# Idle products in four early attention tiles, one evacuation moved up, and Strassen products half a step later, in a fused attention and SwiGLU kernel

## The chip, the cores and the metric

One core of one Trainium2 chip runs the whole program. The metric is the device time of one launch in microseconds. Five launches of the kernel before took 358.25 to 359.82 us, with a median of 358.79 us.

## The reference

The reference is sliding-window attention with a linear bias, followed by a SwiGLU block. There are 8 batches of 8 heads, 576 tokens and 64 channels per head; the block has width 512 and inner width 1536.

```python
scores = scale * q @ k.T
mask = (rel >= 0) & (rel < 128)
scores = where(mask, scores - slope[h] * |rel|, -1e9)
attn = softmax(scores)
x = (attn @ v).transpose(0, 2, 1, 3).reshape(4608, 512)
g = x @ w_gate
out = ((g * sigmoid(g)) * (x @ w_val)) @ w_out
```

## The kernel before

**Work and stages.** The tokens are cut into 36 tiles of 128 queries ("units"): four groups of two batches with nine units each, the ninth unit holding the last 64 tokens of both batches. For a unit, q and k of a 128-token rank are brought into transposed form (`kT`, `qT`), TensorE makes the scores (`products`, L254; L282 for narrow ones), ScalarE takes the exponential (L259, L286), VectorE multiplies by a table that holds both the bias and the mask (L263, L290), TensorE multiplies by v with a column of ones appended (`weighted`, L314), and VectorE divides by the sum (L316, L317). The result is transposed on TensorE (L340) and copied by ScalarE (L341) into `xT`; from unit 24 on a DMA transposes it.

The block then works on nine groups of 512 tokens. For each of twelve slices of the inner width there is a gate product `pg` and a value product `pv` (both L363), a tanh on ScalarE (L374), and two VectorE operations that make `uu` (L376) and `hT` (L380). Group 0 and the last group are projected by plain products (L393, L409). Groups 1 to 7 are projected by a Winograd form of Strassen's method: 7 block products instead of 8. It needs sums of slices of h (`sums`, L451 to L454, VectorE, made from the ninth slice of a group on) and sums of the output weights. Its seven products (L472) come in the order A11·B11, A12·B21, S2·T2, S1·T1, S3·T3, S4·B22, A22·T4; A stands for quarters of h, S for sums of h. Two halves X and Y of one PSUM bank receive six of them; VectorE (`half_plus`, L476) or ScalarE reads a half after the products that complete it. There are two calls of seven products for each group, so 14 calls in all.

**What sets the order.** The head of the program (`first_tiles`: four units, then three slices of group 0 over their first 384 tokens) and the first steps of the block after it are in an order written out by hand for TensorE, VectorE and ScalarE. After that a scheduler orders the instructions of each engine from their priorities. `ffn` counts half steps: number 2m is the gate product of slice m, 2m+1 the value product. The set `AT` says after which half steps of a group one Strassen product of the group before is placed; before, it is 2 to 8 and 10 to 16.

**The head, and what the change touches in it.** The pool with the tag `gv` has three PSUM banks. They are used in turn by the transposed k tiles of the head, by the two halves of `av` of the units 0 to 3, and by the first block products. The transposes of q use one further bank. `REPEAT` gives how often a transposition of a head tile is carried out into the same bank; the repetitions change nothing in the result. `idle` is a piece of zeros in `kT` (L99) that serves as an operand for products whose results are overwritten, `busy(7)` starts the kernel with seven of them (L135). `transposes_to(n)` carries out the transpositions (L201) and evacuations (L206) up to the n-th in a fixed list; the fifth entry of the list, index 4, is q of rank 2, the third q tile. `run(scores(0))` goes through unit 0's steps: 0 is the products, 1 the first exponential, 2 the second one with the first masking multiply, 3 and 4 the same for the other four heads.

**Loads.** GpSimd's queue issues the loads of q, k, v and the weights in one fixed sequence, in which a load waits until the load eight places earlier has landed. From rank 9 on q and k are transposed by DMAs on SyncE's queue (L222).

Of the kernel before, what the change touches and what calls it, by code (L numbers as in the profile page):

```python
# [16 lines left out]
P = 128  # L17
# [6 lines left out]
ENGINES = {"all": None, "compute": {ET.PE, ET.DVE, ET.Activation}, "pe": {ET.PE}}  # L24
WARM = 7
IDLE = {("k", 0): 0, ("q", 0): 2}
REPEAT = {("q", 1): 4, ("k", 1): 4, ("q", 2): 3}
FIRST = 4
LEAD = 6
PRE = 0  # L30
# [4 lines left out]
def slot(h):  # L35

    return 4 * (h // 4) + 2 * (h % 2) + (h % 4) // 2
# [9 lines left out]
def kernel(  # L47
# [10 lines left out]
    nc = tc.nc  # L58
# [30 lines left out]
    def first_masks():  # L89
        nc.vector.tensor_copy(idf, idm)  # L90
        for h in sorted(range(H), key=slot):
            nc.scalar.activation(reg[:, slot(h), :], dist, AF.Exp, scale=-(2.0 ** (-8.0 * (h + 1) / H)))
# [5 lines left out]
    idle = kT[:, NK - 1].rearrange("p j t -> p (j t)")  # L98
# [82 lines left out]
    def transposed(name, rank):  # L181
# [16 lines left out]

        for _ in range(REPEAT.get((name, rank), 2) if rank < FIRST else 1):
            for j in range(4):  # L200
# [25 lines left out]
    def scores(i):  # L226

        s, p = units[i]
        def combined(n):
            return scores_128(s, (3, 7, 8)[n], 8, (s, "c", n), msk[n])  # L230

        def together(one, two):
            return [one[0] + two[0]] + one[1:] + two[1:]

        if p == 8:
            return together(combined(1), combined(2))
        if p == 7:
            return together(scores_128(s, p, p, (s, p), reg[:, :, 0:P]), combined(0))
        if p == 3:
            return scores_128(s, p, p, (s, p), reg[:, :, 0:P])  # L240
        ks = (9 * s + p) % NK
        banks = []
        e = epool.tile([P, H, 256], FP16, name="ex", tag="ex", bufs=4)
        ex[(s, p)] = e

        def products():
            for q4 in range(2):
                two = [ps_a.tile([P, 2, 256], FP32, name="ps", tag="a") for _ in range(2)]
                banks.append(two)
                for j in range(2):  # L250
                    pair = 2 * q4 + j
                    for par in range(2):
                        rows = slice(64 * par, 64 * par + 64)
                        nc.tensor.matmul(two[par][:, j, :], kT[rows, ks, pair, :],  # L254
                                         qT[rows, p:p + 2, pair, :], start=(j == 0), stop=(j == 1))

        def act(q4, par):
            o = 4 * q4 + 2 * par
            nc.scalar.activation(e[:, o:o + 2, :], banks[q4][par], AF.Exp, scale=scale)  # L259

        def mul(q4):
            o = slice(4 * q4, 4 * q4 + 4)
            nc.vector.tensor_mul(e[:, o, :], e[:, o, :], reg[:, o, :])  # L263

        return [[products], [lambda: act(0, 0)], [lambda: act(0, 1), lambda: mul(0)],
                [lambda: act(1, 0)], [lambda: act(1, 1), lambda: mul(1)]]
# [27 lines left out]
    def weighted(i):  # L294

        s, p = units[i]
        x = xpool.tile([P, H, D], FP16, name="x", tag="x")
        xs[i] = x
        for half in range(2):
            pool, tag = (ps_f, "gv") if i < FIRST else (ps_a, "a")  # L300
            av = pool.tile([P, 4, D + 1], FP32, name="av", tag=tag)
            todo = []
            for j in range(4):
                h = 4 * half + j
                if p == 8:
                    for n, kt in enumerate((3, 7, 8)):
                        todo.append((j, ex[(s, "c", n)][:, slot(h), :], va[9 * s + kt][:, h, :]))
                else:
                    if p not in (0, 4):
                        todo.append((j, ex[(s, p - 1)][:, slot(h), 128:256],  # L310
                                     va[9 * s + p - 1][:, h, :]))
                    todo.append((j, ex[(s, p)][:, slot(h), 0:128], va[9 * s + p][:, h, :]))
            for n, (j, w, val) in enumerate(todo):
                nc.tensor.matmul(av[:, j, :], w, val, start=(n == 0), stop=(n == len(todo) - 1))  # L314
            rec = xpool.tile([P, 4, 1], FP32, name="rec", tag="rec", bufs=4)
            nc.vector.reciprocal(rec, av[:, :, D:D + 1])  # L316
            nc.vector.tensor_mul(x[:, 4 * half:4 * half + 4, :], av[:, :, 0:D],  # L317
                                 rec.broadcast_to([P, 4, D]))
# [8 lines left out]
    def x_transposed(i):  # L327
        n, j = place(i)
        if n not in xT:
            xT[n] = bpool.tile([P, NKB, 512], FP16, name="xT", tag="xTc" if n == 8 else "xT",  # L330
                               bufs=1 if n == 8 else 3)
        x = xs.pop(i).rearrange("p h d -> p (h d)")
        dst = xT[n][:, :, j * P:(j + 1) * P]
        if i >= X_DMA_FROM:
            nc.sync.dma_start_transpose(dst, x)
            return
        pool, tag, n = (ps_f, "po", 1) if i < FIRST else (ps_a, "a", 4)
        pt = pool.tile([P, NKB, P], FP16, name="px", tag=tag, bufs=n)
        for kb in range(NKB):
            nc.tensor.transpose(pt[:, kb, :], x[:, kb * P:(kb + 1) * P], idm if i < FIRST else idm2)  # L340
        nc.scalar.copy(dst, pt)  # L341
# [13 lines left out]
    def wide(n, m, which, c1=512):  # L355

        w, ms = wg_sb if which == "g" else wv_sb, slice(m * P, (m + 1) * P)
        ps, c0 = early.pop((n, m, which), (None, 0))
        if ps is None:
            pool, tag = (ps_a, "a") if (n, m, which) in OTHER else (ps_f, "gv")  # L360
            ps = pool.tile([P, 512], FP32, name="p" + which, tag=tag)
        for kb in range(NKB):
            nc.tensor.matmul(ps[:, c0:c1], w[:, kb, ms], xT[n][:, kb, c0:c1],  # L363
                             start=(kb == 0 and c0 == 0), stop=(kb == NKB - 1 and c1 == 512))
        if c1 < 512:
            early[(n, m, which)] = (ps, c1)
        return ps
# [136 lines left out]

    AT = {*range(2, 9), *range(10, 17)}

    def ffn():

        for n in range(NBLK):
# [6 lines left out]
            for m in range(NMB):  # L518
                for half, _ in enumerate(gate_val(n, m)):
                    yield 1.0  # L520
                    if n > 1 and 2 * m + half in AT:
                        next(parts)
# [25 lines left out]
    def transposes_to(n):  # L548
        nonlocal done_t
        while done_t < n:  # L550
            transpose(done_t)
            done_t += 1
# [7 lines left out]
    def run(steps):  # L560
        for fs in steps:
            for f in fs:
                f()
            yield

    def first_tiles():

        first_masks()
        transposes_to(need[0] + 1)
        for n, _ in enumerate(run(scores(0))):  # L570
            if n == 2:
                transposes_to(need[1])
        for i in range(FIRST):
            if i + 1 < FIRST:
                for n, _ in enumerate(run(scores(i + 1))):
                    if n == 0 and i + 2 < FIRST:
                        transposes_to(need[i + 2])
            weighted(i)
            if i > 0:
                x_transposed(i - 1)  # L580

        for m, which in ((0, "g"), (0, "v"), (1, "g")):
            wide(0, m, which, 384)
        x_transposed(FIRST - 1)
        for m, which in ((1, "v"), (2, "g"), (2, "v")):
            wide(0, m, which, 384)

    def attention():

        transposes_to(need[FIRST])  # L590
        for _ in run(scores(FIRST)):
            yield FIRST
        for i in range(FIRST, last + 1):
            if i < last:
                transposes_to(need[i + 1])
                for _ in run(scores(i + 1)):
                    yield i
            weighted(i)
            yield i
            loads_to(i + 7)  # L600
            ahead(i)
            yield i
            x_transposed(i)
            yield i
            yield i + 1
# [110 lines left out]
```

## Time and profile before

| | |
|---|---|
| median of five launches | 358.79 us (358.25 to 359.82) |
| the profiled launch | 360.06 us |
| span of the profile, first to last instruction | 358.3 us |
| outside the span | 1.8 us |
| TensorE busy in the span | 341.1 us, 95% |
| VectorE, ScalarE, GpSimd busy | 271.4, 177.7, 106.9 us |
| idle time of TensorE that a named producer ended, 0 to 26 us | 6.4 us |
| the same, 97 to 345 us | 1.6 us |

The profile counts from the first instruction. PE is TensorE, PEld its weight loads, DVE VectorE, ACT ScalarE, POOL GpSimd and SP SyncE; a q behind a name means the engine's queue, which issues DMAs. A number in square brackets behind a row is the engine's idle time before it, with the producer that ended the idle time. Matmuls are pipelined and their ends are modelled, so starts are more exact than ends.

### The profile page before, as it was taken

How to read it: one execution, taken by the hardware profiler on the slowest of the kernel's cores; microseconds unless marked ns; L12 is line 12 of the kernel's file. 1: busy time of each engine (PE TensorE's matmuls, PEld its weight loads, DVE VectorE, ACT ScalarE, POOL GpSimd, SP SyncE). 2: the span in 40 equal slices, each digit the busy share in tenths (PEclk: the TensorE clock that was granted, in tenths of full speed). 3: DMA queues.
4: the chain of work that ended last, by engine and by line, in shares of the span. 5: the costliest groups of instructions: out<-in, count | busy, mean ns of one | idle time of the engine just before them, and what ended most of it. 6: DMA issues, size and time to landing. Idle time of an engine off the chain costs nothing.

```text
span 358.3 us, 7133 instructions
## 1 busy us (share of the span) xinstructions
PE 341.1 (95%) x2701; PEld 193.8 (54%) x2701; DVE 271.4 (76%) x594; ACT 177.7 (50%) x351; POOL 106.9 (30%) x132
## 2 busy tenths in 40 slices
PE   7788997999999999999999999999999999999995
PEld 3544453444456655665466655654665566456543
DVE  4747975898887699777987998789877955975540
ACT  4726784455656455555565454555554333332321
POOL 8954753466728283664300001000000000000000
PEclk9989999999999999999999999999999999999999
DMA  9999999999999999999962224212021201101104
GB/s 150 171 187 186 171 177 100 147 143 147 167 145 177 163 143 180 170 196 112 170 66 79 42 74 32 78 26 75 15 76 29 75 0 60 59 2 59 59 16 103
DMA packets 159939, 37.87 MB, mean 106 GB/s; under 512 B 150432, under 2 KB 155424, under 8 KB 159904
## 3 DMA queue, kind: packets, MB, share of 16 engines
q0 software_dynamic: 116224, 18.62, 81.8%
q1 hardware_dynamic: 43232, 18.49, 27.7%
q8 instruction: 21, 0.34, 0.4%
q10 hardware_dynamic: 448, 0.30, 0.3%
q14 instruction: 14, 0.11, 0.1%
HBM read 37.91 MB, written 9.44 MB: 132 GB/s over the span
## 4 chain that ended last, share of the span: by engine, by line
PE 76%; DVE 12%; ACT 5%; DMA 3%; issue 2%; SPq 0%; ACTq 0%; DVEq 0%
PE pg L363 23%; PE pv L363 22%; PE po L472 14%; PE ps L254 4%; PE av L314 3%; DVE uu L376 2%; PE po L393 2%; PE p L472 2%; DVE hT L380 2%; DVE ex L263 2%; ACT exc L286 2%; PE px L340 2%; DMA qT<-qn 2%; ACT tt L374 1%; ACT ex L259 1%
## 5 line engine op out<-in xcount | busy, mean ns | idle before, releaser
L374 ACT ACTIVATE tt<-pg 128x512 f16<-128x512 f32 x108 | 64.8, 602 | 108.9 <-PE pg L363 102.9
L363 PE MATMUL pg<-xT,wg_sb 128*128 128x512 f16 (+2 forms) x444 | 116.3, 376 | 1.0 <-ACT xT L341 0.7
L363 PE MATMUL pv<-xT,wv_sb 128*128 128x512 f16 (+2 forms) x444 | 113.8, 375 | 1.2 <-DVE uu L376 1.2
L376 DVE SCALAR_TENSOR_TENSOR uu<-tt,pg 128x512 f16<-128x512 f16 x107 | 73.0, 683 | 39.0 <-ACT tt L374 38.4
L380 DVE TENSOR_TENSOR hT<-uu,pv 128x512 f16<-128x512 f16 x108 | 73.7, 683 | 6.0 <-PE pv L363 2.6
L363 PEld LDWEIGHTS <-wg_sb 128*128 128x128 f16 x444 | 41.8, 98 | 38.6 <-issue 4.4
L363 PEld LDWEIGHTS <-wv_sb 128*128 128x128 f16 x444 | 41.4, 98 | 38.9 <-issue 5.6
L259 ACT ACTIVATE ex<-ps 128x512 f16<-128x512 f32 x96 | 50.0, 608 | 9.5 <-PE ps L254 9.4
L168 POOL DMA_DIRECT2D va<-in_v_dram x40 | 34.3, 868 | 42.0 <-PE av L314 35.3
L174 POOL DMA_DIRECT2D qn<-in_q_dram x39 | 33.6, 864 | 40.2 <-DMA qT<-qn 24.0
L174 POOL DMA_DIRECT2D kn<-in_k_dram x39 | 33.4, 860 | 25.8 <-DMA kT<-kn 21.4
L472 PEld LDWEIGHTS <-hT 128*128 128x128 f16 x336 | 32.1, 98 | 14.9 <-issue 1.0
L263 DVE TENSOR_TENSOR ex<-ex,m_reg 128x1024 f16<-128x1024 f16 x48 | 32.8, 686 | 8.4 <-ACT ex L259 8.3
L472 PEld LDWEIGHTS <-S 128*128 128x128 f16 x252 | 23.9, 98 | 12.7 <-issue 4.1
L317 DVE TENSOR_TENSOR x<-av,rec 128x256 f16<-128x256 f32 x72 | 28.6, 420 | 0.4
L286 ACT ACTIVATE exc<-psc 128x512 f16<-128x512 f32 x40 | 21.0, 603 | 5.7 <-PE psc L282 5.7
L472 PE MATMUL po<-T,hT 128*128 128x256 f16 x168 | 22.9, 272 | 0.1
L472 PE MATMUL po<-T,S 128*128 128x256 f16 x168 | 22.9, 273 | 0.0
L314 PE MATMUL av<-va,ex 128*128 128x65 f16 x384 | 20.7, 193 | 2.2 <-DVE x L317 1.3
L314 PEld LDWEIGHTS <-ex 128*128 128x128 f16 x384 | 18.1, 97 | 6.3 <-DVE x L317 2.0
L254 PE MATMUL ps<-qT,kT 64*128 64x256 f16 x192 | 18.0, 272 | 3.3 <-DMA qT<-qn 1.7
L341 ACT COPY xT<-px 128x512 f16<-128x512 f16 x24 | 14.0, 585 | 12.5 <-PE px L340 12.5
(72 smaller groups left out, 284.0 us busy)
## 6 DMA issues: line engine op xcount, KB each, us to landing
out_dram<-osb SPq DMA_DIRECT2D x32, 256.0 KB, 2.7
va<-in_v_dram POOLq DMA_DIRECT2D x32, 128.0 KB, 8.3
qn<-in_q_dram POOLq DMA_DIRECT2D x31, 128.0 KB, 7.5
kn<-in_k_dram POOLq DMA_DIRECT2D x31, 128.0 KB, 8.4
wo_sb<-in_moe_w_out_dram POOLq DMA_DIRECT2D x2, 768.0 KB, 9.3
wg_sb<-in_moe_w_gate_dram POOLq DMA_DIRECT2D x2, 512.0 KB, 10.5
wv_sb<-in_moe_w_val_dram POOLq DMA_DIRECT2D x2, 512.0 KB, 12.2
out_dram<-osb SPq DMA_DIRECT2D x6, 128.0 KB, 2.3
```

The source lines that it names most:

```text
L168: nc.gpsimd.dma_start(va[rank][p0:p1, :, 0:D], src)
L174: nc.gpsimd.dma_start(t_[p0:p1], src)
L254: nc.tensor.matmul(two[par][:, j, :], kT[rows, ks, pair, :], qT[rows, p:p + 2, pair, :], start=(j == 0), stop=(j == 1))
L259: nc.scalar.activation(e[:, o:o + 2, :], banks[q4][par], AF.Exp, scale=scale)
L263: nc.vector.tensor_mul(e[:, o, :], e[:, o, :], reg[:, o, :])
L314: nc.tensor.matmul(av[:, j, :], w, val, start=(n == 0), stop=(n == len(todo) - 1))
L317: nc.vector.tensor_mul(x[:, 4 * half:4 * half + 4, :], av[:, :, 0:D], rec.broadcast_to([P, 4, D]))
L363: nc.tensor.matmul(ps[:, c0:c1], w[:, kb, ms], xT[n][:, kb, c0:c1], start=(kb == 0 and c0 == 0), stop=(kb == NKB - 1 and c1 == 512))
L374: nc.scalar.activation(tt, pg, AF.Tanh, scale=0.5)
L376: nc.vector.scalar_tensor_tensor(out=uu, in0=tt, scalar=one if (n, m) == PIN else 1.0, in1=pg, op0=ALU.add, op1=ALU.mult)
L380: nc.vector.tensor_mul(hT[n][:, m, :], uu, pv)
L472: nc.tensor.matmul(dst, a[:, m, cols], b[:, m, :], start=(start and m == 0), stop=(m == HM - 1), skip_group_check=True)
```

## The change

It has three parts.

1. In `weighted`, units 1, 2 and 3 get two more products into each of their two `av` banks before the real ones, with the zeros as both operands, 256 columns each: 12 products. Their results are overwritten.
2. In the head, `REPEAT` becomes 2 for k of rank 1 (from 4) and 4 for q of rank 2 (from 3), and q of rank 2 is transposed and evacuated after step 0 of unit 0 instead of after step 2. On TensorE the place stays the same (behind the products of unit 0); on VectorE the evacuation now stands ahead of both masking multiplies of unit 0 instead of between them.
3. `AT` becomes 2, 3, 5 to 9 and 11 to 17: in the first call the two products that use no sums stay, and the other five come half a step later; the whole second call comes half a step later.

```diff
-REPEAT = {("q", 1): 4, ("k", 1): 4, ("q", 2): 3}
+REPEAT = {("q", 1): 4, ("k", 1): 2, ("q", 2): 4}
...
             av = pool.tile([P, 4, D + 1], FP32, name="av", tag=tag)
+            if 0 < i < FIRST:
+
+                for _ in range(2):
+                    nc.tensor.matmul(av.rearrange("p j d -> p (j d)")[:, 0:256], idle[:, 0:P],
+                                     idle[:, 0:256], start=True, stop=True)
...
-    AT = {*range(2, 9), *range(10, 17)}
+    AT = {2, 3, *range(5, 10), *range(11, 18)}
...
         for n, _ in enumerate(run(scores(0))):
-            if n == 2:
+            if n == 0:
                 transposes_to(need[1])
```

In the built programs TensorE's order is otherwise the same up to the first Strassen call; from there the scheduler places both the Strassen products and the attention pieces among the block products differently. The loads up to q of rank 10 and the SyncE queue up to its transposition have the same order in both.

## Prediction

> **What bounds the kernel now.** I read the page first, then the granted clock by windows, then the chain of waits and the TensorE rows of the places it names. The page:
>
> ```profile
> PE 341.1 (95%) x2701; PEld 193.8 (54%) x2701; DVE 271.4 (76%) x594; ACT 177.7 (50%) x351; POOL 106.9 (30%) x132
> PEclk9989999999999999999999999999999999999999
> DMA  9999999999999999999962224212021201101104
> ```
>
> TensorE is the bound, but not everywhere: it idles in the first 26 us, one digit of its clock is below 9, and the DMA engines are full for the first half of the span. The windows (busy time by engine, then clock, DMA share, GB/s):
>
> ```profile
> 17.82:21.24 3.42, 2.04 (x32) 1.32 (x33) 3.23 (x12) 1.61 (x4) 1.82 (x3) 1.00 2.07 169
> 21.24:24.65 3.41, 3.05 (x10) 1.43 (x10) 0.42 (x1) 0.31 (x1) 2.71 (x4) 0.50 1.62 193
> 58.78:62.19 3.41, 1.68 (x11) 0.67 (x10) 0.15 (x1) 1.18 (x2) 2.56 (x3) 1.00 0.62 69
> ```
>
> From 21.24 to 24.65 us the clock was half. VectorE is the busy engine just before (3.23 of 3.42 us). The chain shows what half a clock costs: the same four products of 384 columns,
>
> ```profile
> 23.04 1.28 PE pv L363 x4
> ...
> 26.07 0.65 PE pg L363 x4
> ```
>
> The first row lies in the half-clock window, the second after it: 0.32 us against 0.16 us a product.
>
> The decisive place is later. TensorE's rows (start, duration, what, idle time before and its releaser), and SyncE's queue:
>
> ```profile
> 59.10 0.81 PE L393 MATMUL po<-wo_sb,hT 128*128 128x512 f16 x3
> 61.64 0.27 PE L254 MATMUL ps<-qT,kT 64*128 64x256 f16 x1 [1.73 <-DMA qT<-qn]
> ```
> ```profile
> 53.04 1.30 SPq L222 DMA_TRANSPOSE qT<-qn  x1
> 54.40 1.25 SPq L222 DMA_TRANSPOSE kT<-kn  x1
> 55.84 1.19 SPq L222 DMA_TRANSPOSE qT<-qn  x1
> ```
>
> At 61.64 TensorE stands 1.73 us for q of rank 10, whose DMA transposition was issued at 55.84. The chain names a ScalarE exponential before that issue, but the instruction does not use it: its load was issued at 47.22 and took 8.5 us by the DMA view, so it landed at about 55.7. That load stood in GpSimd's sequence behind others, each released by the landing of an earlier load. So this wait ends at a time that the DMA stream sets, whatever the engines do before it. TensorE runs its instructions in order, and this product stands at the same place in the changed program. I call 61.64 the **join**.
>
> **Part 2, the third q tile.** VectorE's rows:
>
> ```profile
> 9.36 0.42 DVE L206 COPY kT<-pt 128x512 f16<-128x512 f16 x1 [0.47 <-PE pt L201]
> 10.80 0.69 DVE L263 TENSOR_TENSOR ex<-ex,m_reg 128x1024 f16<-128x1024 f16 x1 [1.01 <-ACT ex L259]
> 11.41 0.42 DVE L206 COPY qT<-pt 128x512 f16<-128x512 f16 x1
> ```
>
> The copy at 11.41 waits behind the masking; unit 1's products follow at 11.88, after 1.24 us idle. The transposes themselves take 0.055 us each (12 from 9.80 to 10.64, ends included). Eight fewer of k save 0.44 us, of which unit 0's products can use 0.33 (from 9.26 to 8.93, when the q copy of 8.47 to 8.89 is done); four more of q cost 0.22. They end at 10.64 - 0.33 + 0.22 = 10.53, the copy follows and ends at 10.98, and unit 1's products start at 11.03: **-0.85 us**. The maskings move behind it, to about 11.0 and 11.6; the second ends near 12.3, and its first reader, unit 0's `av` at 13.33, moves to 12.5, so this costs nothing.
>
> **Part 1, the idle products.** 256 columns at 0.86 us / 4 products / 2 are 0.107 us each, 1.28 us for 12. Units 1 to 3 hang on VectorE (its chain from 13.96 to 20.05 has next to no gaps), so most of it lies beside VectorE. One piece does not: four of the products, 0.43 us, come before the narrow scores at 16.88, whose exponential and masking (18.80) are next on VectorE. Those exponentials ended at 18.56 and now end at 18.56 - 0.85 + 0.43 = 18.14, while VectorE is free at 18.80 - 0.85 = 17.95: the masking starts near 18.2, the lead of 0.85 shrinks to 0.6, and the first gate product starts at 21.0 instead of 21.60. Before it, TensorE streamed 1.08 us of columns in the window 17.82 to 21.24 (its rows' columns at 0.42 ns, which is 0.65 us / 4 / 384), 32%, and the clock halved; after the window 58.78 to 62.19, with about 38%, it stayed full. Three of the six pairs fall in the first window, 0.64 us, and bring it to some 50%. So I expect the full clock from 21 to 25: 9.5 products in 3.05 us save 0.16 each, **-1.5 us**. If the half clock stays, this gains nothing, and the four products cost up to 0.4.
>
> Together TensorE leads by 2.1 us at 27. The next obstacle is q of rank 6: issued at 24.67, 13.0 us to landing, so 37.7; its transposes stood at 38.84. The lead is cut to about 1.2 us. Then the join takes all of it: the stall there becomes 1.73 + 1.2 = 2.9 us. **Term of the head: 0.** It costs nothing either if the head gets slower by up to 1.73.
>
> **Part 3, the Strassen products.** No wait for a sum S shows in the groups 2 to 8 (97 to 345 us). What shows is S4·B22 waiting until VectorE has read the other half of the bank:
>
> ```profile
> 124.76 0.38 PE L363 MATMUL pg<-xT,wg_sb 128*128 128x512 f16 x1
> 125.55 0.71 PE L472 MATMUL po<-wo_sb,S 128*128 128x256 f16 x5 [0.41 <-DVE osb L476]
> ```
>
> VectorE's read there (125.08 to 125.50) came after `uu`. Such waits: 0.41, 0.34, 0.41 and five under 0.07, 1.3 us in all; measured from start to start, 0.16 us more for each of the eight, 2.6. In the new order S3·T3 follows a value product: VectorE has `hT` (0.69) to do during the product (0.65), then reads, 0.42; the gate product of 0.86 covers that, and S4 need not wait. But S4 now follows a gate product, so its own read comes behind tanh (0.60) and `uu` (0.69), and A22·T4 behind it takes over the wait S4 had. In the last groups that is a swap, 0.07 for about as much. In the dense groups the scheduler has placed other work in between. The sums' tiles are single, but the next group's are first written after half step 19, and the last S4 is now at 16; no wait comes from there. Ends: -2.6 us if all go and none come, +1.4 if each of the 14 calls gets another 0.1 (1.3 / 14). I take **-0.7**, half of the measured 1.3, as the new order removes one kind and keeps the other.
>
> **Sum.** 358.3 + 0 - 0.7 = 357.6 us of span, with the 1.8 us outside 359.4 for a profiled launch. The profiled launch of before lies 1.3 us over the median, so against the median: 358.79 - 0.7 = **358.1 us**.
>
> **Where a rule speaks against it.** TensorE's rows give half a clock after a window with 32% streamed and none after 38%. The Trainium skill, "TensorE: Matmul & The Clock Gate", section "The HAM clock gate", has the clock halve after an idle window of some 3.4 us, windows running freely. By that rule alone the head, never idle that long, would not have halved its clock, and a stall of 2.9 us at the join would not either: 358.1. By the row it can, and then 359.8. The trace differs from the rule in the head, so the row decides, and the stall is a rival.
>
> **Rivals.**
> - *The stall at the join closes the clock.* Place: 58.7 to 61.64. In before the window there streamed 38%; with 2.9 us idle inside one window of 3.41, at most 0.5 us of columns are left, 15%. The next window, full of block products, would run at half: +3.41/2 = 1.7 us, exposed since nothing but TensorE bounds it. With part 3: 358.79 + 1.7 - 0.7 = 359.8, slower. It decides from about 2.1 us of idle time inside one window (less than 38% streamed). If window borders cut the stall in two parts under 2.1 us, it does not happen; and an unprofiled launch may stall less, being 1.3 us shorter.
> - *The join does not bind in timed launches.* If the recording of 160,000 DMA packets slows that stream, the wait of 1.73 us belongs to the profile, and the lead of 1.2 us stays: 358.79 - 1.2 - 0.7 = 356.9; 355.0 if all of the 2.6 us of part 3 go too. For it: the 1.3 us. Against: the DMA share is full up to 56 us in any case.
> - *Part 3 turns against itself:* A22·T4 and the rearranged attention pieces wait more than S4 did, +1.4: 360.2.
>
> **Chances.** Forecast 0.34, clock 0.30, join open 0.24, part 3 worse 0.12. A measurement of this kernel tells about 0.3%, 1.08 us, from no change. The forecast gives 0.14 faster, 0.18 same, 0.02 slower; the clock 0.01, 0.10, 0.19; the open join 0.23, 0.01, 0; part 3 worse 0, 0.01, 0.11. So faster 0.38, same 0.30, slower 0.32. The range 356.0 to 360.4 takes in the values of all four; beyond it lie only corners such as the open join with part 3's best, or the clock with part 3's worst. The forecast's own, with part 3's two ends, is 356.2 to 360.2.
>
> **What would show it.** Part 2: the copy of q of rank 2 ends near 11.0, unit 1's products at 11.0. Part 1: no half clock from 21 to 25, first gate product near 21.0, four 384-column products in 0.65 us. Head: the stall at the join 2.5 to 3.5 us and its end still 61.6; if the product starts much earlier, the join is not set by the DMA stream and I am wrong by that much. After it: full clock, or the rival. Part 3: waits before S4 gone, new ones before A22; their sum under 1.3 us.

## The result, and the profile after

The changed kernel takes 361.78 us (median of 44 launches, 359.28 to 363.62), the kernel before 358.78 us (79 launches, 357.84 to 362.91). The ratio is 1.0071, with a 95% interval of 1.0059 to 1.0084: slower, by 2.6 us in the means, where I had forecast 358.1. The medians lie 3.0 us apart. The profiled launch took 361.62 us, with a span of 359.8 us.

The page of the changed kernel. The granted clock now has its dip in the eighth slice of 9 us, from 63 us on, and none at 21 to 25 us:

```profile
PE 341.6 (95%) x2709; PEld 194.5 (54%) x2709; DVE 272.3 (76%) x594; ACT 177.0 (49%) x351; POOL 106.9 (30%) x132
PEclk9999999899999999999999999999999999999999
PE 70%; DMA 12%; DVE 6%; ACT 4%; POOL 3%; issue 3%; ACTq 0%; DVEq 0%; POOLq 0%; SPq 0%
```

The last line is the chain of waits by engine: 12% of it is DMA, where the kernel before had 3%. The page gives the parts: 6% and 3% are loads of weights, 2% a load of q, and 2% the transposition of q, as much as before. Ahead of the join the chain now goes through the loads and no longer through the engines.

The head did what the prediction worked out. VectorE's rows (the third q tile, then both maskings in one row), and TensorE's first products of unit 1 and first gate products:

```profile
10.43 0.43 DVE L206 COPY qT<-pt 128x512 f16<-128x512 f16 x1 [1.26 <-PE pt L201]
10.77 1.28 DVE L263 TENSOR_TENSOR ex<-ex,m_reg 128x1024 f16<-128x1024 f16 x2
```
```profile
10.91 0.50 PE L254 MATMUL ps<-qT,kT 64*128 64x256 f16 x5 [0.52 <-DVE qT L206]
...
20.83 0.81 PE L368 MATMUL pg<-xT,wg_sb 128*128 128x384 f16 x4 [0.67 <-ACT xT L346]
21.48 0.81 PE L368 MATMUL pv<-xT,wv_sb 128*128 128x384 f16 x4
```

The copy ends at 10.86 (before: 11.83), unit 1's products start at 10.91 (11.88), the first gate product at 20.83 (21.60), and four products of 384 columns start 0.65 us before the next four. What came of it is in the windows (busy time of the engines, then granted clock, DMA share and GB/s) and in TensorE's rows:

```profile
21.09:24.51 3.42, 3.42 (x26) 2.12 (x25) 0.00 (x0) 0.59 (x1) 2.72 (x4) 1.00 1.68 190
58.64:62.05 3.41, 0.15 (x1) 0.09 (x1) 0.00 (x0) 0.56 (x1) 0.64 (x1) 1.00 1.14 73
62.05:65.46 3.41, 3.41 (x9) 1.19 (x9) 0.75 (x1) 0.60 (x1) 3.41 (x5) 0.50 1.06 67
```
```profile
57.75 0.81 PE L398 MATMUL po<-wo_sb,hT 128*128 128x512 f16 x3
61.90 0.27 PE L254 MATMUL ps<-qT,kT 64*128 64x256 f16 x1 [3.34 <-DMA qT<-qn]
62.10 1.89 PE L368 MATMUL pg<-xT,wg_sb 128*128 128x512 f16 x4
...
65.48 1.03 PE L368 MATMUL pg<-xT,wg_sb 128*128 128x512 f16 x4
```

At the join TensorE stands 3.34 us instead of 1.73 us, and gets q of rank 10 no earlier than before (61.90 against 61.64). The window around the stall holds 0.15 us of work; the next one runs at half the clock, four products in 1.68 us (62.10 to 63.78) instead of 0.86.

Four marks, in us, show where the lead of the head is lost:

| | before | after | difference |
|---|---|---|---|
| first gate product | 21.60 | 20.83 | -0.77 |
| first product of group 0's projection | 56.83 | 55.48 | -1.35 |
| first product of rank 10's scores (the join) | 61.64 | 61.90 | +0.26 |
| first Strassen product | 97.95 | 99.41 | +1.46 |
| end of the span | 358.29 | 359.84 | +1.55 |

In this pair of launches the half clock costs 1.2 us: from the join to the first Strassen product it is 36.30 us before and 37.51 after. From there to the end it is 260.34 and 260.43 us, so part 3 neither gave nor took more than 0.1 us. This table explains 1.5 us. The medians are 3.0 apart because the profiled launch of before was itself a long one: its span of 358.3 us lies above most of its launches, which the next section takes up.

### The profile page after: what moved, and what is told of

The parts are those of the page before. It is cut to its first block, busy times and chain, and to the rows that moved or that the text cites. A ratio compares the mean times of both kernels' runs of the same rounds, so it can differ in the third digit from the quotient of the medians.

```text
span 359.8 us, 7142 instructions
## 1 busy us (share of the span) xinstructions
PE 341.6 (95%) x2709; PEld 194.5 (54%) x2709; DVE 272.3 (76%) x594; ACT 177.0 (49%) x351; POOL 106.9 (30%) x132
## 4 chain that ended last, share of the span: by engine, by line
PE 70%; DMA 12%; DVE 6%; ACT 4%; POOL 3%; issue 3%; ACTq 0%; DVEq 0%; POOLq 0%; SPq 0%
PE pv L368 21%; PE pg L368 21%; PE po L477 14%; DMA wv_sb<-in_moe_w_val_dram 6%; PE po L398 4%; PE av L319 3%; PE ps L254 3%; DMA wo_sb<-in_moe_w_out_dram 3%; PE p L477 2%; DMA qn<-in_q_dram 2%; DMA qT<-qn 2%; ACT ex L259 2%; DVE hT L385 2%; DVE uu L381 1%; PE px L345 1%
## 5 line engine op out<-in xcount | busy, mean ns | idle before, releaser
L319 PE MATMUL av<-va,ex 128*128 128x65 f16 x384 | 20.5, 193 | 0.5
```

## The experiments

Ratios are to the kernel before, timed on the same chip; they are worked out from all launches, so a median and its ratio can differ. "Transposition" is the time from the issue to the landing of the DMA transposition of q of rank 10, "packet" the start of a record that the trace's DMA packets have about every 256 TensorE instructions (products and weight loads): one packet of 16 KB of instructions, which takes about 0.9 to 2.3 us.

**Which part is it?** `at_only` is part 3 alone, `head_only` parts 1 and 2.

```diff
at_only
-    AT = {*range(2, 9), *range(10, 17)}
+    AT = {2, 3, *range(5, 10), *range(11, 18)}
head_only: the changed kernel with
-    AT = {2, 3, *range(5, 10), *range(11, 18)}
+    AT = {*range(2, 9), *range(10, 17)}
```

> The kernel before with part 3 alone (the new AT). Theory J (the join: the lead of the head becomes a longer stall at 61.6 us, and the stall halves the clock for a window): no lead, so the stall at the join stays at up to 1.7 us, no new half-clock window after it, and the time falls by 0.3 to 0.7 us: 358.1 to 358.5. Rival P (part 3 is the loss): slower by 2 us or more, about 361, with the loss spread over the groups 2 to 8.

> The kernel changed without part 3 (parts 1 and 2 alone). Theory J: stall at the join of 3.0 to 3.5 us, a half-clock window behind it, slower than before by 2.5 to 3.2 us: 361.3 to 362. Rival P: no slower than before by more than 0.5 us.

at_only: 359.86 us, ratio 1.0025 (1.0001 to 1.0049). head_only: 361.84 us, ratio 1.008 (1.0054 to 1.0105). The head alone makes the whole loss. at_only has not the gain expected, and its own loss of 0.25% only just clears no change; where that lies is open. From the first Strassen product to the end the profiles have 260.42 and 260.36 us, beside 260.34 of before, so a loss of at_only is not in the products that it moves, and rival P is refuted. head_only stands 3.64 us at the join and has the half clock behind it. at_only's profiled launch shows the opposite case: the clock was half for two windows in the head (20.88 to 27.7), TensorE came late, and did not wait at all:

```profile
61.67 0.28 PE L254 MATMUL ps<-qT,kT 64*128 64x256 f16 x1
```

Its transposition took 4.17 us, that of before 5.66.

**Which half of the head?**

```diff
evac_only: before with
-REPEAT = {("q", 1): 4, ("k", 1): 4, ("q", 2): 3}
+REPEAT = {("q", 1): 4, ("k", 1): 2, ("q", 2): 4}
...
-            if n == 2:
+            if n == 0:
                 transposes_to(need[1])
idle_only: before with
+            if 0 < i < FIRST:
+                for _ in range(2):
+                    nc.tensor.matmul(av.rearrange("p j d -> p (j d)")[:, 0:256], idle[:, 0:P],
+                                     idle[:, 0:256], start=True, stop=True)
```

> The kernel before with part 2 alone: the third q tile is evacuated ahead of the maskings, k of rank 1 repeated 2 times and q of rank 2 4 times, no idle products, AT as before. Theory J (the lead of the head runs into the product of rank 10's scores, whose operand a DMA transposition delivers at 61 to 62 us; the longer TensorE stands there, the more often the clock is halved behind it): part 2 moves the first gate product forward by 0.6 to 0.85 us at most, the half-clock window in the head can still come; the lead at 57 us is under 1 us, so the stall grows from 1.7 to at most 2.6 us; the time lies between before and the head alone: 359.0 to 360.5. Rival I (the idle products are the loss, they delay TensorE or feed the join; the early evacuation is harmless): no change or a gain of up to 0.85, 358.0 to 358.8. Rival E (the early evacuation alone makes the loss): 361.8, as the head alone.

> The kernel before with part 1 alone: twelve idle products of 256 columns in units 1 to 3, all else as before. Theory J: the full clock from 21 to 25 us saves about 1.5 us, the four products ahead of the narrow scores cost up to 0.4, so the lead at the join is over 1 us and the stall 2.5 to 3 us, enough for a half-clock window behind it: 360.5 to 361.8. Rival I (the idle products are the whole loss): 361.8. Rival E (the loss is the evacuation's): 358.0 to 359.0. J and I are told apart by the other run, with the evacuation alone, and by the stall's length in this one's profile.

evac_only: 358.79 us, ratio 0.999 (0.9969 to 1.0011). idle_only: 360.79 us, ratio 1.0043 (1.002 to 1.0067). The early evacuation alone is harmless and gains nothing that can be measured, as rival I said; the idle products lose. evac_only leads by 1.3 us at the projection (55.52), as the changed kernel does, and still stands only 0.91 us at the join, since its transposition took 4.15 us and landed at 59.37. idle_only stands 3.00 us for one that took 5.36 us. So the lead alone does not make the long stall: the transposition differs. The DMA view from 57.5 to 61.5 us (busy share in 40 slices), first of the changed kernel:

```profile
DMA  9332211112599999990000000100000799991000
GB/s 26 19 19 22 20 18 26 38 36 31 26 261 128 261 266 269 190 3 0 0 0 0 0 5 5 10 8 10 10 10 10 154 289 287 287 241 11 0 0 0
```

and of evac_only:

```profile
DMA  9999999699991000000000000000005376999999
GB/s 80 182 202 284 259 274 44 144 287 292 294 247 3 0 0 0 0 0 0 0 0 0 0 0 0 0 0 0 0 0 164 26 50 41 65 91 129 141 129 143
```

In evac_only the transpositions run through to 58.7 us, and the instruction packet follows at 60.55, in the slice with 164 GB/s. In the changed kernel the packet starts at 58.63; from 59.2 to 60.6 next to nothing moves, and the transpositions end only then.

**Is it the join?** Two ways to take it out: a product that is overwritten, for which the scheduler places the scores of rank 10 some five block groups later (`_pad`), and an order of the loads in which q of rank 10 comes before half of the output weights (`_wo`).

```diff
after_pad, before_pad
+                if i == 9 and q4 == 0:
+                    nc.tensor.matmul(two[0].rearrange("p j q -> p (j q)"), idm2,
+                                     reg[:, 0:2, :].rearrange("p h q -> p (h q)"),
+                                     start=True, stop=True)
after_wo, before_wo
-    for a0 in (0, 6):
+    def load_wo(a0):
...
+    load_wo(6)
...
+            if loaded == 12:
+                load_wo(0)
```

> The changed kernel with one more product (constant operands, 512 columns, 0.22 us) at the head of unit 9's score products; its result is overwritten. In the built order that one takes the early place, and all eight real score products stand behind five groups of block products, 4.3 us later. Theory J: the stall at the join (3.3 us in the profile after) and the half clock behind it go, the head's lead of 1.4 us arrives at the end; 361.8 - 3.3 - 1.7 to 3.4 + 0.2 = about 356 to 357. Rival K (TensorE only stands at the join because something behind it is late anyway): another wait takes its place within the next 5 us, and the time stays above 360.

> The kernel before with the same one product at the head of unit 9's scores. Theory J: the stall there (1.7 us in the profile of before; perhaps less in other launches, since that launch was 1.3 us over the median) goes: 357.0 to 358.5, and 1 to 2 us over the changed kernel with the same product, as the head's lead now counts. Rival K: no gain, 358.8 to 359.

> The changed kernel with one DMA moved: of the two loads of the output weights, the one of rows 6 to 11 stays where it was and the one of rows 0 to 5 is issued after the loads of rank 11, so that q of rank 10 is loaded, and transposed, about 4 us earlier. TensorE's work is the same. Theory J: no stall over 1 us at rank 10's scores, no half clock behind it, and the lead of the head (about 2 us at 27 us, 1.2 after q of rank 6) can be kept up to the next transposition that is late, near 72 us: 357.0 to 358.8, at least 2.5 us under the changed kernel. Rival K (the stall only moves to the next transposed tile or to the output weights that now land later, with the same loss of clock): 360.5 to 362. Rival L (the loss does not lie at the join at all but in the order of the products after it): 361.8, with no stall in the profile.

> The kernel before with the same one DMA moved. Theory J: the stall of 1.7 us at rank 10's scores goes, but the clock did not halve behind it in the profile, so the gain is at most the stall less what the next transposition takes back: 357.3 to 358.8. Rival K: 358.8 or a little more, with a new wait for output weights or the next rank. If it is faster than the changed kernel with the same DMA moved, the change has a cost of its own beside the join.

after_pad: 360.29 us, ratio 1.0019 (0.999 to 1.0048); before_pad: 358.07, 0.9982 (0.9963 to 1.0001). after_pad's median is not the 356 to 357 of theory J but in rival K's range, and before_pad's is in theory J's range, though its interval holds no change too. Without the stall at the join most of the loss goes, but in part of the launches it returns: after_pad's spans are 355.5 to 358.4 us in six launches and 358.6 to 361.5 in the other six. The next transposition, k near 72 us, is then the one that TensorE waits for (0.78 us in the profiled launch). The changed load order failed: after_wo 360.99, 1.0055 (1.0029 to 1.008), before_wo 360.01, 1.0021 (0.9993 to 1.005). after_wo now stands 4.0 us for the output weights that were put back, and the transposition got slower instead of earlier (7.88 us; before_wo 6.11). So this pair says only that the join can't be opened this way.

**Is it the packet?** The packet comes at a rough count of instructions: in all 20 profiled launches the one in question started when TensorE had started 479 to 511 products, and 489 products stand ahead of the join in before, 497 in the changed kernel, 485 in evac_only. The count is not exact: before's own three launches had 487, 489 and 498. So I moved it by products whose results are overwritten or repeated. `_f27` cuts the idle products at the start of the kernel into more and shorter ones with the same columns, 27 more products; after_m14 has 14 products fewer.

```diff
after_f27, before_f27
-        for _ in range(n):
-            nc.tensor.matmul(t_, idle[:, 0:P], idle, start=True, stop=True)
+        for _ in range(4 * n):
+            nc.tensor.matmul(t_[:, 0:P], idle[:, 0:P], idle[:, 0:P], start=True, stop=True)
...
-            for _ in range(IDLE[(name, rank)]):
-                nc.tensor.matmul(pt.rearrange("p j t -> p (j t)"), idle[:, 0:P], idle,
+            for _ in range(4 * IDLE[(name, rank)]):
+                nc.tensor.matmul(pt[:, 0, :], idle[:, 0:P], idle[:, 0:P],
after_m14
-REPEAT = {("q", 1): 4, ("k", 1): 2, ("q", 2): 4}
+REPEAT = {("q", 1): 4, ("k", 1): 1, ("q", 2): 3}
...
-                for _ in range(2):
-                    nc.tensor.matmul(av.rearrange("p j d -> p (j d)")[:, 0:256], idle[:, 0:P],
-                                     idle[:, 0:256], start=True, stop=True)
+                bank = pool.tile([P, 512], FP32, name="av", tag=tag)
+                nc.tensor.matmul(bank, idle[:, 0:P], idle, start=True, stop=True)
...
```

> The changed kernel with the same idle columns at its very start cut into more products: the seven products of 512 columns become 28 of 128, and the two of 512 ahead of the first q tile become eight of 128, so that TensorE has 27 more products and 27 more weight loads before anything else, and the same work behind them. Theory F (the records of the DMA engines show a 16 KB packet of TensorE's instructions about every 256 instructions; with the change TensorE gets to one of these points at 58.4 to 59.0 us, while the transposition of q of rank 10 is under way, and it then takes 5.4 to 5.7 us from issue to landing, against 4.15 to 4.17 in the two runs whose packet came after it): the packets come 27 products earlier, the one in question near 55 us; the transposition takes about 4.2 us, lands near 60.3, the stall at rank 10's scores is 1.5 to 2.2 us instead of 3.3, no half clock behind it, and the time falls to 358.5 to 360.0, unless the packet's new place delays the transpositions ahead of it as much. Rival T (the packet only coincides; the transposition is slow because its data or the traffic of other loads is late): the transposition again takes 5.4 us or more, the stall is 3 us, the time 361 to 362. Up to 0.4 us can be lost in both by the shorter products at the start.

> The kernel before with the same cut of the idle columns at the start, 27 more products and weight loads. Theory F: transposition of q of rank 10 at about 4.2 us, landing near 60.1, stall under 0.8 us, time at or a little under before's, 357.5 to 359.0. Rival T: landing at 61.3 or later, and no difference of time.

> The changed kernel with 14 products fewer ahead of rank 10's scores: each pair of idle products of 256 columns becomes one of 512 (the same columns), q of rank 2 is transposed three times instead of four and k of rank 1 once instead of twice; the loads keep their order. Rank 10's scores are then TensorE's product 483 or so, instead of 497; the instruction packet came in all looks while TensorE was between its products 479 and 510. Theory F (the packet inside the transposition makes it 1.4 us slower): the packet comes behind the scores, as in the run with the early evacuation alone; the transposition takes 4.2 us and lands near 60.3, the stall is 1.5 to 2.0 us, the clock stays full in most launches, 358.3 to 360.0. Rival T (the transposition is late for another reason, and it was the shift at the start that helped): 5.4 us or more, landing at 61.5, a stall of 3 us, 361 to 362.

after_f27: 359.01 us, ratio 1.0 (0.9975 to 1.0025). The loss of the changed kernel (1.0071, 1.0059 to 1.0084) is gone, though all its real work is still there, in the same order. The packet started at 56.21, ahead of the bulk of the transpositions' data, and q of rank 10 took 4.45 us. TensorE's rows of after_f27:

```profile
58.12 0.81 PE L398 MATMUL po<-wo_sb,hT 128*128 128x512 f16 x3
60.49 0.27 PE L254 MATMUL ps<-qT,kT 64*128 64x256 f16 x1 [1.56 <-DMA qT<-qn]
60.69 1.04 PE L368 MATMUL pg<-xT,wg_sb 128*128 128x512 f16 x4
```

The stall is 1.56 us and the clock stays full behind it. Each timed launch has its mean granted clock on record, and a window at half the clock takes about 0.005 off it: 10 of after_f27's 12 launches have a mean of 0.998 or more, so no such window, of the changed kernel's 44 only 8. after_m14: 359.61, 1.0021 (0.9993 to 1.005); in the profiled launch the packet came behind the join, at 60.84, the transposition took 4.18 us:

```profile
57.54 0.81 PE L398 MATMUL po<-wo_sb,hT 128*128 128x512 f16 x3
59.74 0.27 PE L254 MATMUL ps<-qT,kT 64*128 64x256 f16 x1 [1.39 <-DMA qT<-qn]
```

Half of its launches have spans of 356.4 to 356.8 us, as this one, the other half 358.8 to 361.1. before_f27 was to gain up to 1 us by the theory and did not: 359.34, 1.001 (0.9984 to 1.0036). Its packet ran from 56.5 to 58.8, again inside the transposition, which took 5.77 us. A shift by a fixed number hits or misses, as the issue of the transposition moves too, between 55.16 and 56.84 us in these launches.

**Does the count do it alone?** evac_f7 and before_f7 have seven products more at the start, and nothing else.

```diff
evac_f7, before_f7
-        for _ in range(n):
-            nc.tensor.matmul(t_, idle[:, 0:P], idle, start=True, stop=True)
+        for _ in range(2 * n):
+            nc.tensor.matmul(t_[:, 0:256], idle[:, 0:P], idle[:, 0:256], start=True, stop=True)
```

> The early evacuation alone, with the seven idle products of 512 columns at the start cut into fourteen of 256: rank 10's scores become TensorE's product 492 instead of 485; the work and its times are the same. Theory F: the instruction packet now falls ahead of the scores in most launches, at 58.5 to 59.5 us, the transposition takes 5.4 to 5.7 us, the stall is 2.3 to 2.7 us and the time rises from 358.8 to 360.0 to 361.5. Rival L (only the lead counts, the number of products does not): 358.8 again, with a landing near 59.5.

> The kernel before with the same cut: rank 10's scores become product 496 instead of 489. Theory F: launches with the packet inside the transposition become more frequent, and the time rises by 0.5 to 2 us, to 359.3 to 361. Rival L: 358.8.

evac_f7: 359.32 us, ratio 0.9995 (0.9963 to 1.0026): not what theory F said. before_f7: 360.25, 1.0022 (0.9993 to 1.005): the median is in the range expected, but the interval holds no difference too. In both profiled launches the head ran at half the clock for two windows, TensorE came late, and the packet came as the data of the transposition ended or later (at 62.38 us in evac_f7, 60.42 in before_f7; transpositions of 4.26 and 4.30 us). So the number of products alone did not decide in these two launches; TensorE's lead matters too. How much of each, these runs leave open.

**The kernel before, twice more.** Unchanged, for the profile alone.

> The kernel before once more, for a second profile. Its profiled launch was 1.3 us longer than its median. Theory F and J: in a launch near the median, with a span of 356 to 357 us, rank 10's transposition lands about 60 us (4.2 us after its issue) with the instruction packet after it, or the head had its full clock; if the launch again has a span above 358, the packet is at about 59.3 us and the landing at 61.5. Rival T: a short span with a landing at 61.5 and a packet at 59.3 us would say that the stall of 1.7 us is in every launch and the spread comes from elsewhere.

> The kernel before, a third profile; the two so far had spans of 358.3 and 360.7 us, above the 356.9 of its median. Theory F and J: if the span is 356 to 357.3, the transposition of q of rank 10 takes 4.2 us or the stall is under 1.2 us; if it is above 358, a packet at 58.8 to 59.5 us and a landing at 61.5 again. Rival T: a span under 357.3 with a landing at 61.5 and a stall of 1.7 us or more.

before_again took 362.5 us, with a span of 360.7 us: the kernel before can have the changed kernel's fate by itself. Its head happened to have the full clock, TensorE was at the projection at 55.71, the packet started at 58.86, and (TensorE's rows, then windows):

```profile
57.99 0.81 PE L393 MATMUL po<-wo_sb,hT 128*128 128x512 f16 x3
61.66 0.37 PE L254 MATMUL ps<-qT,kT 64*128 64x256 f16 x1 [2.86 <-DMA qT<-qn]
```
```profile
21.09:24.51 3.42, 2.75 (x21) 1.71 (x22) 0.94 (x3) 0.74 (x2) 2.73 (x5) 1.00 1.59 194
58.64:62.05 3.41, 0.55 (x3) 0.20 (x3) 0.00 (x0) 0.73 (x2) 1.23 (x2) 0.82 0.92 72
62.05:65.46 3.41, 3.41 (x9) 1.20 (x10) 0.75 (x1) 0.60 (x1) 3.41 (x5) 0.50 1.39 93
```

A stall of 2.86 us, and half the clock for two windows: 38.74 us from the join to the first Strassen product. before_third (359.86 us, span 358.1) had two half-clock windows in the head, a late TensorE, a transposition of 4.28 us and no stall. None of the three profiled launches of before was one of the common ones, whose spans are near 357 us, so no profile shows their transposition. The spans tell something of it. From the join to the end every profile with the scores in their old place and the full clock behind the join takes 296.6 to 296.7 us, so a span of 357.0 puts the join near 60.4, 1.3 us before the profiled one. With an issue near 55.84, and 0.13 us from landing to product as in the profile, that is a transposition of about 4.4 us: an estimate.

The timed launches can be sorted by their mean granted clock, into those with no, one and two half-clock windows (0.998 or more; 0.993 to 0.995; 0.989 to 0.991). The launches of before are the 145 timed beside the experiments, on three chips; two of them had three windows.

| half-clock windows | before: launches, median span | changed kernel: launches, median span |
|---|---|---|
| none | 63, 357.0 us | 8, 358.1 us |
| one | 59, 357.2 us | 23, 359.8 us |
| two | 21, 358.3 us | 13, 361.3 us |

So the changed kernel is 1.1 us longer even in launches that keep the full clock, and has a half window in 36 of 44; in before the first half window costs next to nothing. Where the window lies is recorded for the profiled launches alone.

**Does a version beat both?**

> The changed kernel with both: the idle columns at the start cut into 27 more products, and one more product of 512 columns, overwritten, in rank 10's score bank, for which the scheduler places the eight real products some five block groups later. Theory F with J: rank 10's transposition lands near 60.3 and its products stand near 63, no stall; what remains of the lead of the head (1 to 2 us) is kept or waits at the next transposition near 72 us: 357.0 to 358.5, under the kernel before. Rival M (the next transposition or the packet's next place takes it back, with a half-clock window in many launches, as in the run with the pad alone): 359.5 to 360.5.

> The kernel before with the same two edits. Theory F with J: as for the changed kernel, but with the head's own loss left in (up to 1 us at the join, where the half-clock window falls into the head): 357.5 to 358.7. If the changed kernel with these edits is not below this one, the head's gain is lost in every arrangement tried. Rival M: 359 to 360.

> The changed kernel with 27 more products at the start and the overwritten product of 512 columns in the score banks of rank 10 and of the rank after it; for the second the scheduler moves nothing, so it only adds 0.2 us of work ahead of a product that may wait. Theory F with J: as with one pad, 358.0 to 358.8. If the next transposition binds in many launches, the second product is hidden there; where it does not, it costs 0.2 us.

The edits are those of `_f27` and `_pad` together; in after_pad2_f27 the condition is `i in (9, 10)`. after_pad_f27: 358.42 us, ratio 0.9993 (0.9967 to 1.0019). before_pad_f27: 359.58, 1.0007 (0.998 to 1.0033). after_pad2_f27: 359.48, 0.9997 (0.9964 to 1.0031). None can be told from before; after_pad2_f27 missed its 358.0 to 358.8, and before_pad_f27 lies in rival M's range. What is left is the next transposition; of before_pad_f27:

```profile
PE ps L258 <- DMA kT<-kn: 2.6, 1, 2.6
```

with half the clock behind it from 74.8 us. In after_pad_f27 that wait was 0.2 us, and the span 355.6.

## Why the prediction was wrong

**Where it failed.** The step "so this wait ends at a time that the DMA stream sets, whatever the engines do before it". It ends with a DMA, and the loads do set when the transposition is issued; but its length depends on where TensorE's own packet falls in that stream, and the sooner TensorE comes, the more often it falls into the transposition. Of the 18 launches with the loads in their old order, the four that began group 0's projection at 57.6 us or later all had the packet at the end of the data or behind them; of the nine earlier ones without the 27 added products, seven had it inside. In these 18, the transposition of q of rank 10 took

| packet of 16 KB starts | launches | issue to landing |
|---|---|---|
| at 56.5 to 59.3 us, between issue and landing, before the data are through | 9 | 5.36 to 5.77 us |
| at 60.4 us or later, when the data are through | 6 | 4.15 to 4.30 us |
| at 55.3 to 56.2 us, up to 0.5 us behind the issue | 3 | 4.12 to 4.45 us |

Against the forecast for a profiled launch, 359.4, the 361.62 measured are 2.2 us too long: within rounding 0.3 at the join, 1.2 of half clock and 0.8 of part 3, which is below. Against the forecast for the median, 358.1, it is 3.7; most of the rest is the 1.3 us by which before's profiled launch lies above its median.

From the failed step come the wrong size of two terms:

- *Term of the head: 0.* I carried the profiled launch's stall of 1.73 us over to all launches, as if every launch of before had it. The row was right, but the launch had the packet at 59.30 and a transposition of 5.66 us. The 1.3 us by which it lay above the median was the sign; I used it as a constant offset. In a launch with 4.2 us, a lead is paid back at once when the packet turns it into 5.6 us. Between medians this is about 1.1 to 1.4 us of the 3.0: 1.1 between the spans of launches without a half window, 1.4 between the rows of the table above. It is an estimate, since no common launch of before was profiled.
- *The stall closes the clock.* This was my first rival, and its mechanism and place came true: stall 3.34 us, half a clock from 62.05. Its price was 1.2 us in the profiles, not 1.7, and where the other 0.5 us of the half window came back was not traced. Between the changed kernel's launches with no, one and two half windows it is 1.7 and 1.5 us, but those may differ in the stall too. Its chance of 0.30 was too low: I set 2.1 us of idle time as the point, and the forecast's own 2.9 us was past it. In the launches here, stalls of 0.91, 1.39, 1.56, 1.73 and 2.50 us left the clock full, those of 2.57 (before_pad_f27), 2.86, 3.00, 3.34 and 3.64 us went with half a clock. The length alone does not decide, though: as the prediction had it, what counts is the idle time inside one window. Half the clock begins at 60.81 in before_again and 60.82 in idle_only, so 2.0 and 2.1 us of their stalls lay ahead of it; the 2.50 us of before_f27 (58.60 to 61.10) are cut into 1.1 and 1.4 us by a border at 59.70, counted back in steps of 3.41 us from its clock's change at 356.65. So up to 1.73 us of a stall in one window left the clock full, and 2.0 us halved it. The prediction's 38% for before's window at the join is small: its rows come to 41%, which puts the point near 2.0 instead of 2.1 us. The Trainium skill, "TensorE: Matmul & The Clock Gate", section "The HAM clock gate", asks for an idle window of about 3.4 us. The rows differ from it: 2.0 us of idle time in one window were enough here.

**Part 3, -0.7.** Measured +0.1 us, from the first Strassen product to the end. The waits before S4 went, 1.2 us to 0.2 us in the waits from 97 to 348 us (first of before, then of the changed kernel):

```profile
PE po L472 <- DVE osb L476: 1.2, 3, 0.4
```
```profile
PE po L477 <- DVE osb L481: 0.2, 1, 0.2
PE po L477 <- ACT p5s L495: 0.6, 2, 0.3
PE p L477 <- ACT exc L286: 0.4, 1, 0.4
```

Others took it back, and the swap that I described was the small part of them. A22·T4 waits for VectorE's read at two places, 0.14 and 0.07 us. The larger ones were in no term: S3·T3, now behind a value product, stands twice for ScalarE's read of the half that S1·T1 filled (`p5s`, 0.31 us each), and A12·B21, whose bank comes from a pool that attention uses, waits 0.4 us for an exponential. I counted half of the wait as gained; nothing in the profile stood for that half.

**What was right.** Part 2: 0.97 us gained at unit 1's products (0.85 predicted), the copy's end at 10.86 (10.98). Part 1: the full clock from 21 to 25 us, the first gate product at 20.83 (21.0), a lead of 1.35 us after q of rank 6 (1.2), a stall there of 0.74 us. But even this was the gain of one launch: the head of before has the full clock in one of its three profiled launches and two half-clock windows in another, so the 1.5 us are not the change's in every launch.

**The rivals.** "The join does not bind" is refuted for the changed kernel and holds for some launches of others; a lead kept would have been 356.9. The 0.2 us between before's launches with no and with one half window speak against it too: a faster head is worth next to nothing there. The range ended at 360.4 because I took forecast and rival as two cases with one stall; that before's typical launch has a shorter transposition was in none of them.

## What to carry to other kernels

Before a lead is counted as lost or kept at a transfer, ask what moves that transfer's end, the stalled engine's own instruction packets included, and profile the kernel before more than once: one launch that lies above its median may show the very stall that the others do not have. A stall of the bound engine of which about 2 us fall into one window of the clock costs twice, its length and then 1.2 us or more per window of half clock behind it. Filler products that keep the clock in one place move the instruction packets and the leads in every later place, so they are to be tested at the next join, not where they stand.

## What the hardware showed that I had not expected

- One packet of instructions, 16 KB, holds up a DMA transposition by about 1.4 us when it falls into it (table above); in the changed kernel at most 10 GB/s moved from 59.2 to 60.6 us. The Trainium skill, "Runtime: NRT & Kernel Launch", section "Instruction fetch mechanics", has instructions refilled in blocks of 16 KiB, 256 instructions, at a cost that is mostly hidden. The trace agrees with the size and the count (21 packets in about 5,400 products and weight loads); here the cost is not hidden from the transposition beside it, nor from TensorE where that waits for the transposition.
- The window of the clock has no fixed place in the kernel. Before's three profiled launches have half a clock at 21.24 to 24.65, at 60.8 to 67.6, and at 20.5 to 27.3 us. The Trainium skill, "TensorE: Matmul & The Clock Gate", section "The HAM clock gate", says that the windows run freely; the three launches agree with that. Here the windows differ in place and number between launches of one program, and with them the span.
